# A new order, new engines and new buffers for the same tasks: attention and a gated feed-forward on one core

## The chip, the core and the metric

The kernel runs on one core of a Trainium2 chip. The metric is the time of one execution in microseconds of the device; lower is better. A core has a matrix engine (PE in the profile, with its weight loads as PEld), VectorE (DVE), ScalarE (ACT), GpSimd (POOL) and SyncE (SP), which here only issues transfers. Each works through its own queue of instructions in order; semaphores order them against each other.

## The reference

Four batches of eight heads, 768 positions, head size 64. Heads 0, 2 and 6 see all earlier positions, the other five see 4 first positions and a window of 64. What follows is a gated feed-forward over the 3072 tokens:

```
scores = (q @ k.T) / sqrt(64), masked; a = softmax(scores); attn = a @ v        # per batch and head
x = attn, heads side by side: 3072 x 512
g = x @ w_gate; val = x @ w_val                                                # 512 -> 1536
out = (g * sigmoid(g) * val) @ w_out                                           # 1536 -> 512
```

## The kernel before

The program is cut into 1155 tasks, each a handful of instructions for one engine. Three long strings, planned beforehand, fix everything that the tasks leave open: `ORDER` is the order in which they are issued (so the order in every engine's queue), `WAYS` says for each task which of its allowed engines runs it, and `SLOTS` which buffer of a ring it takes. `Plan.order` reads them:

```
numbers = [DIGITS.index(ORDER[2 * i]) * 62 + DIGITS.index(ORDER[2 * i + 1])
           for i in range(len(ORDER) // 2)]
for t, w in zip(self.tasks, WAYS):
    t.way = t.ways[int(w)]
```

Two numbers in `ORDER` that are no tasks stand for filler matmuls of PE. The eight banks of 512 fp32 that the matmuls write to are one ring for everything: a task's slot is its bank, and it must wait until whoever reads the bank's last tenant is done.

The tasks that the rest speaks of, with the lines under which the profile has them:

- `load q3`, `load x2`, `load g4`: SP fetches 512 KB of q, of v (it is called x) or of a weight into a raw buffer (L352 to L365). `cq`, `ck`, `cx2.0.1`, `wc g4` cast them to 16 bits (L209 on ScalarE, L211 on GpSimd, L215 on VectorE); `cx2.m.j` are the four quarters of one v buffer. Values are kept in tile `vt`.
- `sc5.2`, `ex5.2`, `mask5.1`, `val5.1`, `nm5`: for tile 5 of 128 queries, a unit of scores on PE (matmuls over 64 rows, L570), its exponential on ScalarE (L582), the multiplication by a 0/1 mask (L590, VectorE or GpSimd, two operands in SBUF), the product with the values (PE, L600), the division on VectorE (L607, L608). `sk`, `sv` copy a few rows of keys and values; `tr`, `ev`, `xtr`, `xe`, `dk`, `dq`, `xdma` are transposes and their copies.
- `gate4.3.0`, `tanh`, `vals`, `stt1`, `stt2`: for group 4 of 512 tokens and column block 3 of 12, the gate product (4 matmuls of 512 columns, L762), tanh on ScalarE (L768), and on VectorE the two products that make h (L775, and L781 or L1152). For groups 4 and 5 the val product is made with seven products instead of eight (`wp5.2.4v` are 4 matmuls of 256 columns, L1108), which are put together by `wy` (copies), `wb` (VectorE, L1129) and `wa` (GpSimd or VectorE, L1129).
- `out4.p1` to `out4.p7`: the output product of a group with seven block products (12 matmuls of 256 columns each, L866), again with sums around it. `hs4.x.part` are the sums of blocks of h (L837, 128x768 at 16 bits, both operands in SBUF, VectorE or GpSimd); `oe4.r1`, `c11`, `r6`, `r67`, `r56`, `c12`, `c21`, `c22` gather the products from the banks into `out_sb` (L904, most on VectorE, each adding to what an earlier one left). `st` are the stores.

What each sum of h reads and writes decides who waits for whom:

```
to, a, b, op = {1: (s1, A[1, 0], A[1, 1], ALU.add),
                2: (A[0, 0], s1, A[0, 0], ALU.subtract),
                3: (A[1, 0], A[0, 0], A[1, 0], ALU.subtract),
                4: (A[0, 1], A[0, 1], A[0, 0], ALU.subtract)}[x]
```

`out5.p5` needs both parts of `hs5.1`, `out5.p6` both of `hs5.2`; `hs5.3.1` needs `hs5.1.1`, and `hs5.2.1` needs `hs5.3.1`. The sums for group 4 must have been read before those of group 5 are written.

Of the kernel before, what the change touches and what calls it, by code (L numbers as in the profile page):

```python
# [14 lines left out]

ORDER = (
    "06000307090A01081U1V0D041cxl1W1X0C021d1f0B20211g1e280g1i2229231h2B2A1j0m1r2C0h1Y1p1s2D1a0F1Z2N1q"
    "2X1b2E0G2O051k1l2W1t1m2F1u2L1x1v1w2f2M1n2g1y2cxk2h0n27252d241o262l2i2e2m2G0E0y2H1z2I2P0z2j2Q8m2t"
    "2R0k8w8n102o308x8o2x112p2U312J0i132V8p2K8z2y0H8q918y2k9G928r3C2n94939L2z8s3I9H323D0q9B95968t149I"
    "8u3J903L978v389C0l99983K9D9E0j2Z9M9A9J3M9F2Y9O9N0o3N9K3U339P1C3V3R2a2q2r0I3S2b9p2s16343O2u3W9k9q"  # L20
    "0r3T3P9r35363b9l2v0J3E379V3X3F1D3H3f3i3Q9Q9m3g0s1F9n9R9W3A3h9S9u0p399o9s9v3B9X2w0K9z179t3j0x3Y9w"
    "3Z0M193u9Y3a3G3l9Z3n3c3m9a1G0uA09T3v9bA13o3d0t409U3k2SA23e9c0O43A33p441A3q41459x3r2T0v42490L9y4C"
    "463y4D9f4H4A3w3x9i9g4B479d9h0P9j3s124Q4K3t4N4R9eB74O1HB24LA6BA48B8B5A7B30QB9184EAd4M0w5C1Q4ZBM15"
    "4F4PBBBP4g4G1BAsA8B40RAYAtB60N4YAxAu1KBNAvA94e5D1IBC1RBO1TAeAgAyAf1J5GATAwBD0SB0Az1EBQ5KAUBH4VAh"
    "4I1MBFBE4h5fA4BG1SAZ0T5EAa5IAi1L5FB1AbBI1OAV4J4aAnAc4bBJAC0VA5AB4fAoAA4d4l4o1NAD5gBK1P3zAG4p5nAE"
    "BL4m4S0aAH4TAjAI5JAp4WAk4U4i5L4q4jAM4v4c4n0W4rAJ5H514y4XANAK4zAF5l4k52AWAL4sAO4tAlAS4u4w0U5T54AX"
    "5m5UAq535055APAr6LAm5W565MAQ57BTBRARBU5o5NBV58BW5c594x5XBf5ABS5O5B5v5p5s5Y5w5VBh5q0YBX5t0XBY5Z5r"
    "5a0ZBd5i5b606366Be64BZ6H676w5P6I6N5QCj6K5uCUBaCk6P6EClCPBcCVBg0bCKCQCW745dCm5R7OCLCF73Cn5hBi69CN"
    "5SCMCR5x5yCOC06O615zCXC16J5e6vC2C3685kBq0f6x6572BjBrCYCGC46Q6ACIBl7P5jCHBt71Bs8e6U6RBk6VCe0eBu0c"
    "CA6WCf626SCg6B6CCJChCB6TCCBvCiCSBw6DBb70C5Bx6G6eCTByC66yBpC77F6X6Z0d7GBzC86YCZ7HC96a757CCa6n6FCb"  # L30
    "Bm6o817Q6b6c76CqCDCs826dDf7DBnCc77BoDr7E89CEE1Ds7WDt7879E2DcCdDu7XCrDdE3CtE4De7UDD7A6MCo6gDvDE7L"
    "7RDgDmDF7BCuE5DGDnCp7VDXCvDHDoDI88DYDZ6z7Y6k7bDJ7S6lDKDS7ZDa6m7j7IDb7JDTDp8f7K7cE6Dq6fDU6p7m6hE7"
    "E8E96i7dDN80EA6jDL6q86Dw7M7a7N6r6sDxDOD06t7nDy6u7p7eD1Cw7x7fDM7q8387DP8A7T8D7sCx8ED2Cz7gD3DV8B7o"
    "DhDW7h7rD47i7t7kDiEaD68NDj85D5Cy8G8YD87u8ZD7DQEc8H7vDR8I8W7y7wEtDk8J8C8X8F8T8QDl8K8L8g8UDzEb8hEu"
    "Ee8O7l8RFNE0EfEv7z848i8jD98MDC8VEg8kF0EhDAElEi8SDBEmFl8lEj8PF1EwF8Fm8aEEExFnEG8bEk8cFpEdF98dEpFq"
    "EnEBF2FrEoFAEyEqF4FBEDEzErF3FCEsECFRFsFFFSF5GcFGEFFtFDFTEHFOEJFoFPFZGYEKFUF6FaEIFEF7FVFbGjFQGZFW"
    "ENFcGdGaFuFXFJFvGeGbFYFdFKGfFxFHFeEOFLFwFyGnFfGkEMGrFIGgGsG1FzGlGhHPG2FMGiG0FhG3GtFgFiEPGoHQGuGm"
    "HLELEQGvHRGpH6GqG5FjERFkHSH7HjG6G4ESH8HkH2G7GwETHlHMG8GxEVGyH3HTGzHNH0EWHUEUEZHOHrHVGCH1HmHvH9HW"
    "HsHnGBEXHtHXHoHwHpHDGEH4HqHYHbEYHxHEGDHHH5HcHAHfHuHBHyHFHCHZG9HIHgHdHGGHGFHhHJHaHzGGHKGLGKI0HeGA"
    "GRGIGJI1HiI3I2I9GNI4GMI5GPI6IBGOGUGSIAGQI7GVGTGWINICI8GXIEIDIRIFIHISITIJIGIIILIKIOIUIMIQIXIVIPIa"  # L40
    "IWIYIZIbIc"
)
WAYS = (
    "000000000000000000000000000000000000000000000000000000000000222222202202202021110101101110110120"
    "212101100000000000000000210012022201011011000000000000002100222212001010000000000001001000000000"
    "001200002221000000001001000000001000010010000000000212210100000000010000002000000100000120010010"
    "000000000100000001200000000000000000000000000000000000000000220000001000000000100000210001001000"
    "002101120020000001001000000021000100100000000021020000000000000000010001202200200000001000000002"
    "100000000000012001020000000000000000000200000000000000001100010000000000000000000000000000000000"
    "000000000000000000000000000000000000000000000000000010000010000000000000000000000000000000000000"  # L50
    "000000000000000000000000000000000000000000000001100000000000000000000000000000000000000000000000"
    "000000000000000000000000000100011100100000000000001000000000000000000000000000000000000000000000"
    "000000000000000001001110001000000000001110110000000001000000000000010000000100000000100000000000"
    "000000000000000000000000000000000000000000011110000110000000000010111100000100001000000000000000"
    "000000000000000000000000000000000000000000000000000000000000000000000111000110000000011001011001"
    "000"
)
SLOTS = (
    "00142310557834204A728958195847A05075426281030677515371900124020502261616103140412010360010742002"
    "230141644162600102323204501403026420412050167244160200630522202002012065012304614540136200140030"  # L60
    "240446501210360010203640541636200124622522240461410021100360646216225204112036102200040230524011"
    "754000311261110210650104126300270103022210611241110500540131010000035544525102202260017123601001"
    "134116402151200027401451273542323411351124127310321226025402571046015210141134122541546421225110"
    "511741244025511051263100312340064001500410070060289507A26253604307171403041416110712161035452396"
    "8A20102627386131505051406140110030713108323248"
)
# [1277 lines left out]
```

## Time and profile before

| | |
|---|---|
| time, three runs | 236.64 us median (236.51 to 236.7) |
| span of the profiled execution, first to last instruction | 234.7 us |
| PE busy | 228.7 us, 97% |
| VectorE busy | 204.4 us, 87%; 51.04 of 53 us from 165 to 218 us |
| ScalarE busy | 157.9 us, 67% |
| GpSimd busy | 136.4 us, 58% |
| granted PE clock | 0.999 |

The page gives no other time of the profiled execution than its span; the 1.9 us between span and median lie before the first and after the last instruction of the program. A matmul's duration holds the filling of the array, so consecutive matmuls overlap in the records, and a PE that is busy throughout can still start its matmuls late; the starts tell how densely they are issued.

### The profile page before, as it was taken

What the parts mean: (1) busy time and instruction counts of PE and PEld (TensorE: products, weight loads), DVE (VectorE), ACT (ScalarE), POOL (GpSimd) and SP (SyncE); (2) the same over time, 40 slices, a digit from 0 to 9 for tenths busy, and PEclk for the clock granted to TensorE, in tenths of its full rate; (3) what the DMA queues carried; (4) which work ended last, traced back from release to release, by engine and by line L of the source; (5) the groups of instructions that cost most, each with busy time, mean ns of one, the idle gap of its engine ahead of it and who ended that gap; (6) DMA issues with size and microseconds to landing.
All of it is one profiled execution on the core that took longest, in us unless ns stands there. A gap on an engine that the chain in (4) does not pass through costs nothing.

```text
span 234.7 us, 5854 instructions
## 1 busy us (share of the span) xinstructions
PE 228.7 (97%) x2283; PEld 152.8 (65%) x2283; DVE 204.4 (87%) x369; ACT 157.9 (67%) x256; POOL 136.4 (58%) x150
## 2 busy tenths in 40 slices
PE   7899999999999999999999999999999999999994
PEld 2577865654457778645564556776876767668883
DVE  1889989989989998989879974889979999999954
ACT  3599999679899779856786389768554643553110
POOL 7485499864695300469840887273096930593950
PEclk9999999999999999999999999999999999999999
DMA  6999999999999998998994621500920000220054
GB/s 180 351 343 366 327 340 369 343 341 314 271 259 220 236 251 166 270 179 178 234 217 124 102 45 31 62 3 2 225 45 3 3 0 3 89 89 4 0 201 159
DMA packets 67196, 40.76 MB, mean 174 GB/s; under 512 B 25184, under 2 KB 61024, under 8 KB 67168
## 3 DMA queue, kind: packets, MB, share of 16 engines
q1 hardware_dynamic: 65104, 37.37, 64.5%
q10 hardware_dynamic: 2064, 3.02, 3.6%
q8 instruction: 18, 0.29, 0.5%
q14 instruction: 10, 0.08, 0.1%
HBM read 28.31 MB, written 6.29 MB: 147 GB/s over the span
## 4 chain that ended last, share of the span: by engine, by line
PE 89%; ACT 3%; DMA 2%; DVE 2%; SPq 2%; issue 1%; POOL 0%; ACTq 0%; POOLq 0%
PE banks L762 45%; PE banks L866 23%; PE banks L1108 8%; PE banks L570 6%; PE banks L600 6%; DMA raw<-in_k_dram 2%; ACT e L582 2%; SPq L352 1%; PE banks L476 1%; PE banks L624 1%; DVE xb L608 1%; ACT kT L209 0%; SPq L357 0%; DVE kT L211 0%; DVE sil L775 0%
## 5 line engine op out<-in xcount | busy, mean ns | idle before, releaser
L762 PE MATMUL banks<-xt,wg_sb 128*128 128x512 f16 (+1 forms) x304 | 71.6, 368 | 0.1
L582 ACT ACTIVATE e<-banks 128x1024 f16<-128x1024 f32 (+2 forms) x68 | 59.4, 911 | 11.0 <-PE banks L570 6.3
L768 ACT ACTIVATE sig<-banks 128x512 f32<-128x512 f32 (+1 forms) x76 | 42.8, 577 | 30.6 <-PE banks L762 23.2
L762 PE MATMUL banks<-xt,wv_sb 128*128 128x512 f16 (+1 forms) x208 | 48.2, 363 | 0.0
L762 PEld LDWEIGHTS <-wg_sb 128*128 128x128 f16 x304 | 28.6, 98 | 25.9 <-issue 0.5
L866 PEld LDWEIGHTS <-h_sb 128*128 128x128 f16 x420 | 40.2, 98 | 7.4
L775 DVE SCALAR_TENSOR_TENSOR sil<-sig,banks 128x512 f32<-128x512 f32 (+1 forms) x52 | 32.8, 641 | 5.8 <-ACT sig L768 4.7
L781 DVE SCALAR_TENSOR_TENSOR h_sb<-sil,banks 128x512 f16<-128x512 f32 (+1 forms) x52 | 32.8, 640 | 3.1 <-PE banks L762 2.7
L837 POOL TENSOR_TENSOR h_sb<-h_sb 128x768 f16<-128x768 f16 x13 | 21.3, 1644 | 21.1 <-DVE hs_sb L837 17.2
L762 PEld LDWEIGHTS <-wv_sb 128*128 128x128 f16 x208 | 19.1, 98 | 17.2
L590 POOL TENSOR_TENSOR e<-e,m 128x640 f16<-128x640 f16 (+1 forms) x16 | 26.6, 1670 | 5.7 <-ACT e L582 4.7
L904 DVE TENSOR_TENSOR out_sb<-banks,out_sb 128x512 f32<-128x512 f32 x37 | 25.0, 684 | 2.1 <-PE banks L866 1.7
L866 PE MATMUL banks<-wt_sb,h_sb 128*128 128x256 f16 x216 | 26.0, 273 | 0.1
L866 PE MATMUL banks<-wo_sb,h_sb 128*128 128x256 f16 x204 | 24.9, 273 | 0.0
L209 ACT COPY raw<-banks 128x512 f32<-128x512 f32 x26 | 14.6, 588 | 15.2 <-DVE h_sb L1152 5.5
L570 PEld LDWEIGHTS <-kT 64*128 64x128 f16 x472 | 14.5, 94 | 9.2 <-issue 8.7
L570 PE MATMUL banks<-qT,kT 64*128 64x128 f16 x472 | 19.9, 218 | 0.1
L211 POOL CAST hq<-raw 128x1024 f16<-128x1024 f32 (+1 forms) x9 | 8.0, 893 | 20.1 <-DMA raw<-in_k_dram 18.2
L600 PEld LDWEIGHTS <-e 128*128 128x128 f16 x472 | 17.3, 97 | 3.6 <-POOL e L590 0.3
L600 PE MATMUL banks<-vt,e 128*128 128x65 f16 x472 | 18.6, 193 | 0.0
L608 DVE TENSOR_TENSOR xb<-banks,rc 128x512 f16<-128x512 f32 x24 | 16.6, 691 | 0.8
L775 DVE SCALAR_TENSOR_TENSOR banks<-sig,banks 128x512 f32<-128x512 f32 x24 | 16.3, 687 | 0.2 <-ACT sig L768 0.2
(85 smaller groups left out, 318.6 us busy)
## 6 DMA issues: line engine op xcount, KB each, us to landing
raw<-in_v_dram SPq DMA_DIRECT2D x12, 512.0 KB, 6.8
raw<-in_q_dram SPq DMA_DIRECT2D x8, 512.0 KB, 5.6
...
```

Source lines behind the costliest of these rows:

```text
L570: nc.tensor.matmul(sc[:, c:c + n, :], weights, moving, start=first, stop=last)
L582: nc.scalar.activation(out=to, in_=src, func=AF.Exp, scale=scale)
L590: ENG[task().way].tensor_tensor(out=ev, in0=ev, in1=mm, op=ALU.mult)
L600: nc.tensor.matmul(avs[t][:, odd, n * 66:n * 66 + 65], ee, vv, start=(m == 0), stop=(m == len(bl) - 1))
L608: nc.vector.tensor_tensor(out=xb.rearrange("p n o d -> p o n d"), in0=av[:, :, :, 0:64], in1=rc.to_broadcast([128, 2, 4, 64]), op=ALU.mult)
L762: nc.tensor.matmul(ps, wsb[:, kk, j * 128:(j + 1) * 128], xt[:, kk, c[0]:c[1]], start=(kk == 0), stop=(kk == 3))
L768: nc.scalar.activation(out=sg[g, j, c], in_=gs[g, j, c], func=AF.Tanh, scale=0.5)
L775: nc.vector.scalar_tensor_tensor(out=sl[g, j, c], in0=sg.pop((g, j, c)), scalar=1.0, op0=ALU.add, in1=gs.pop((g, j, c)), op1=ALU.mult)
L781: nc.vector.scalar_tensor_tensor(out=hs[g, j][:, c[0]:c[1]], in0=sl.pop((g, j, c)), scalar=0.5, op0=ALU.mult, in1=vs.pop((g, j, c)), op1=A ...
L837: ENG[T_hs[g, x][part].way].tensor_tensor(out=to, in0=a, in1=b, op=op)
L866: nc.tensor.matmul(rooms[g, p][:, x, lo:hi], left[:, j, 128 * x:128 * x + 128], right[:, j, lo:hi], start=(on is None and (j == 0 if apart ...
L904: nc.vector.tensor_tensor(out=cell(*to), in0=room, in1=plus, op=ALU.add)
```

## The change

All 1155 tasks and the 9 filler matmuls stay; what each computes stays. Of the 1155 tasks 146 change their engine, 502 of the 622 buffers are another one, and the order changes everywhere from the 151st entry on. Sums with two operands in SBUF: 27 go from VectorE to GpSimd and 29 from GpSimd to VectorE. The diff is three strings; its first lines:

```
-    "2X1b2E0G2O051k1l2W1t1m2F1u2L1x1v1w2f2M1n2g1y2cxk2h0n27252d241o262l2i2e2m2G0E0y2H1z2I2P0z2j2Q8m2t"
+    "2X1b2E0G2O051k1l2W1t1m2F1u2L1x1v1w2f2M1n2g1y2czY2h0n27252d241o262l2i2e2m2G0E0y2H1z2I2P0z2j2Q8m2t"
...
-    "8u3J903L978v389C0l99983K9D9E0j2Z9M9A9J3M9F2Y9O9N0o3N9K3U339P1C3V3R2a2q2r0I3S2b9p2s16343O2u3W9k9q"
+    "8u3J903L978v9C99989E389O0o3K9A2Z9D9F0J9M3M2Y2q2r9N9P3N332s3R0l0r9J342a3S9K2u1C169p9q9r3W3X3F3O2b"
```

Read as names, these are the pieces that the text below needs. The first 150 entries keep their order, except that the 72nd, a filler of 4 matmuls, writes another bank (7 instead of 0); near the start the engines change: before the first gate ScalarE gains `sv0.1` (from GpSimd) and `xe0` (from VectorE), and gives `evq2.0` to VectorE and `cx1.1.0` to GpSimd.

PE around the first score units of tiles 5 and 6, where `|` stands where 64-row score matmuls begin or end:

```
before: vals0.2.256 vals0.3.0 vals0.3.256 | sc6.2 sc5.2 sc6.1 | val4.1 val4.0 gate0.9 | sc6.0 sc6.3 | gate0.8
after:  vals0.2.256 vals0.3.256 val4.1 val4.0 | sc5.2 sc6.1 | vals0.3.0 gate0.9 | sc6.3 sc6.0 sc6.2 | gate0.8
GpSimd before: sk0.3 cx2.0.1 cx2.0.0 wc_g4 cx2.1.1 wc_g2
GpSimd after:  wc_v1 cx2.0.1 cx2.0.0 cx2.1.0 wc_g4 wc_g2
```

The loads up to `load x3` are issued in the same order as before. From the first gate on, PE changes to 64-row score matmuls and back 25 times before and 23 times after.

The end, from the last split products on:

```
PE before: out4.p1 out4.p2 wp5.2.3v gate5.10 out4.p6 out4.p5 gate5.11 out4.p7 out4.p4 out4.p3 out5.p1 out5.p5
           out5.p2.0 out5.p6 out5.p7 out5.p4 out5.p2.1 out5.p3.0 out5.p3.1
PE after:  out4.p1 wp5.2.5v gate5.4 gate5.5 gate5.10 wp5.2.3v out4.p2 wp5.2.4v gate5.11 out4.p5 out4.p7 out4.p6
           out4.p3 out4.p4 out5.p1 out5.p5 out5.p6 out5.p7 out5.p4 out5.p2.1 out5.p3.0 out5.p3.1 out5.p2.0
VectorE before: stt1_5.10 stt2_5.5 stt2_5.10 oe4.r6 stt1_5.11 stt2_5.11 oe4.r67 oe4.r56 oe4.c21 oe4.c12 oe4.c22
                hs5.3.1 hs5.2.1 hs5.2.0
VectorE after:  wb5.2.c12v stt1_5.10 stt2_5.10 stt1_5.4 stt2_5.4 stt1_5.5 stt2_5.5 stt1_5.11 stt2_5.11 oe4.c11
                hs5.1.1 oe4.r6 oe4.r67 oe4.r56 oe4.c12 oe4.c21 oe4.c22 hs5.2.0 hs5.2.1 oe5.r1 hs5.4.0 hs5.4.1
GpSimd before:  hs4.4.1 hs4.4.0 hs5.1.0 hs5.3.0 hs5.1.1 hs5.4.0 hs5.4.1
GpSimd after:   hs4.2.0 wa5.2.c11v hs4.2.1 hs4.4.1 hs4.4.0 hs5.1.0 hs5.3.0 hs5.3.1
```

The last product is then `out5.p2.0`, gathered by ScalarE (`oe5.c11.0`, 256 columns) and stored from ScalarE's queue; before it was `out5.p3.1`, gathered by VectorE and stored from SP's. Banks at the end, after: `out5.p1` takes banks 2 and 3 (bank 3 had `out4.p7`), `out5.p5` takes 6 and 7 (they had `out4.p3` and `out4.p4`).

In VectorE's queue a task stands right behind one whose result it reads 19 times before and 54 times after; from `wp4.1.1v` on (the first split product) 9 and 24 times.

More of the change, by code (lines that the diff above doesn't have):

```diff
@@ L21 @@
[L21 to L40, printed above, removed]
@@ L41 @@
-    "IWIYIZIbIc"
+    "8u3J903L978v9C99989E389O0o3K9A2Z9D9F0J9M3M2Y2q2r9N9P3N332s3R0l0r9J342a3S9K2u1C169p9q9r3W3X3F3O2b"
+    "3P3U9k3T0I35363b9l3E371D9V3V179W9m9Q0j3H3f9X3i3j3g390p0u9n9o9s9T3Q9t3Y3Z0K9R3v9S9Y1F9zA03a3k9U3l"
+    "3h1GA1193n3u3o0x9Z4344A2A39u3c9v0t3m9x452v2w9w9y400O3G1A413A3B423p8e3q3r9a2S46494C9b9c9d9e0L4A4D"
+    "474H9f9g3s2T3t3d3e3z9i9h9jA64Q4R1H0s0N4N4O483x0w4K4VAd0vAeA7AxAf154LBCBD0M5C3wAyBFBEBG3y4B4YAzBM"
+    "AgA90TAhBNBOBP5J0P1EBQ4eB74E0c4F1O4f4G12BHBIBJ1M1N181Q1R4P4ZB8BAB94gAvB0BKBBBL0S1B1I0Q4IAsAt0R4M"
@@ new lines @@
+    "B1B2Au5i4JB3Ai4dATAUB55D5LAw1P5KAV4S0b4T4UB4B6AjA4A5AlAkAm5gAWAX1JA84W4i4o4p4l4hAn1TAYAZAq4XAA0Y"
+    "4aAaAbAc1KAoApAr4vAC4jABAD4m4n5fAG5152AH5H4q4r5n5T1SAI0U5U1L4b4k4s4c5IAJ4t4u5l53AK4y4zAL5M5455AF"
+    "AM0WAE5W5cAO56576MBR50AP5XBT8gBU4w5F58BV5hBX59ANAQ7P4x5ABZ5N0XASBS5vBW5p5q5wAR8f5s605t5EBY5V5Y6H"
+    "BfBdBaBe5B0a6v5oCUCVCW5rCFCGCHBvBgBw0ZCICJBx0VC5C65mC7C8C9716N6OByBz5O5P725Q5RC0C1C3C2C45G5Z5a5b"
+    "CX7T6w5uCjCm8h5j0e6I6P6670CY69Bc63CkCl6ECn5k7Q6465CZCaCPCQCA67CRCbCcCd0dBqCD5d685x6ACBCCBrBs5y61"
@@ new lines @@
+    "6Q736x5zCEBtBuCeCfCg6R6S0f74Bb5S6UCKCL62CMBhBi6V7X6B6C7O8k8lCS6D5e6e6G6n6oCT6X7F7U7G6T816KChCi6J"
+    "BjBl6Y6W6Z6a7C75CN6FCOBmBk6b6c8088DcCrBnCq76DdDIDeDf7HDg7D7E6dBoDJDK77DrDLDsE66y78Dt84DME1E27LDp"
+    "797AE7E9BpE8EAE37RDm6gDnDwCs85Do7W6k7V6l7YDuDv6f7ZDxDyCoCu6h6iDq7b7jCwCpCx6z7ICtCv8iDS7J7KE47ME5"
+    "7cDD7dDTDU7S6p8786DEDF7m6q7p896m6j7N7xD0D1D2D36L6r6s6t6uD4Cy7n8D8A7q7eD57fDz8NE07a7B7g7h7i8EDXDY"
+    "DV82DW8BDaDZDND67sDbDO7rDP7k8Y7t8G8F7oDh7u7vCz8Z7wDGDHEtEaEu8j8H8I8JD88C8T8UEcEbEdEeElEfDkDQEmEv"
@@ new lines @@
+    "DR83F0D7EgEwDiExF8F9DjEnDlF1FFFGDC7y8K8L8OF2D9EhFAEi8MEjDAFB8QEDEy8R7lDB8WEpEqEk8VFCFJFHEzF38XEE"
+    "FDErFVFWEsFKFXFYFNFOEo7zFZFaFPFQG5FLFMG6G78SF4FEFIFtFb8a8b8cFdF5FpFeFuFcFf8PFRG8FSFTEBECFvEJEGEI"
+    "EFFq8dFUEKGcGdF6FgFrF7FwFxFsFhFiFyFzGjEHELERGkFjFkGYG0EMENEPEOG1G2GZGbGrGsHPFlFmG3G4GtHQGeEQFnET"
+    "EUHLGuGlGaGvFoGfGwGgGhH2ESEVGyH3H6HMGzGiHNHRGBGmHSGnH7GoHjHkEWHlHDH8H4HOGpH5GDEZH9HAHvHwHTGqH0Hm"
+    "HUEXHxHyEYGCGEHEGxHVH1HWHXHBHrHnHsG9GFHtHFHuGGHYHZHHHIHoHpHqHaHbHfHzI0HJHKGHGKI1I2HcHCHdHGHeI3GJ"
@@ L42 @@
+    "GRHgHhHiGNI4I5I6GLGAGII9IAGMGOGUGSGVGWIBGPGQI7ICGTGXINIDIEI8IHIFIGIJILIIIUIKIOIQIMIPIVIWIXIYIaIb"
+    "IZIcIRISIT"
 )
 WAYS = (
[L44 to L52, printed above, removed]
@@ L53 @@
-    "000000000000000001001110001000000000001110110000000001000000000000010000000100000000100000000000"
-    "000000000000000000000000000000000000000000011110000110000000000010111100000100001000000000000000"
-    "000000000000000000000000000000000000000000000000000000000000000000000111000110000000011001011001"
+    "000000000000000000000000000000000000000000000000000000000000222102222002222200221011000000100000"
+    "222101100000000010000000220002022222011011000000000000001100222222011010000001000001001000000000"
@@ new lines @@
+    "002101002121000000000000000000020000000000000000000202100100000000010000002000100000000120002200"
+    "000000000000000002100000000000000022102200000010000000001000210002022000000100000000220000001000"
+    "001201011200000001000000000021000000000000000220020000000100000000010000102002220000001001000000"
+    "100000000000021001000200000000000000000020001001000000001011111100000000000000000000000000000000"
+    "000000000000000000000000000000000000000000000000000001010000000000000000000000000000000000000000"
@@ new lines @@
+    "000000000000000000000000000000000000000000010001100000000000100000000000000000000000000000000000"
+    "000000000000000000000000000000110000000000000000011000000000000000000000000000000000000000000000"
+    "000000000000000011111110010000000000000010100001000000000000100010000100000001000000000000000000"
+    "000000000000000000000000000000000000000000011111100110000000000001101100000000000000001000000000"
+    "000000000000000000000000000000000000000000000000000000000000000000001101100000000000001001010000"
@@ L58 @@
 SLOTS = (
[L59 to L65, printed above, removed]
+    "193204751A36723497219A6737716025547A6945821014A096350A004124202206015603340323626444120430610445"
+    "616041230245613146341000364022025503410002426532002320550421511343226420121005323322025061151140"
+    "031521335026104400123032520516004543545260410322210241102021343110533141232510255136061540230518"
+    "920411750255004101321070025711311024012210371147004301720237125702246747040121601770107100010141"
+    "252003101210160121012071267067645212661113002200560131000512720044127312770173002067520120030014"
+    "70257110212340257011011711261127600051146415307137522443205A606115100403141112110602071245371617"
+    "46506373515A4021405171305131403020610027951461"
 )
```

## The prediction

> **What bounds the kernel now.** I read the first lines of the page, then the busy time by stages, then the chain of work that ended last.
>
> ```profile
> span 234.7 us, 5854 instructions
> PE 228.7 (97%) x2283; PEld 152.8 (65%) x2283; DVE 204.4 (87%) x369; ACT 157.9 (67%) x256; POOL 136.4 (58%) x150
> ...
> 20.00:66.00 46.00, 46.00 (x477) 28.12 (x476) 43.32 (x86) 41.21 (x67) 33.22 (x38) 1.00 1.13 331
> 165.00:218.00 53.00, 53.00 (x418) 38.68 (x416) 51.04 (x87) 26.13 (x48) 29.90 (x22) 1.00 0.17 47
> 218.00:232.00 14.00, 13.40 (x122) 11.66 (x120) 10.87 (x19) 1.56 (x3) 8.10 (x6) 1.00 0.34 122
> ...
> 203.53 3.45 PE banks L762 x16
> 218.30 13.11 PE banks L866 x120
> ```
>
> In the stage rows the numbers after the length are PE, weight loads, VectorE, ScalarE and GpSimd. From 20 us to the last matmul PE is busy throughout, at a granted clock of 1.00. The two pieces of the chain say how densely: 16 matmuls of 512 columns in 3.45 us are 0.216 us each, 120 of 256 columns in 13.11 us are 0.109 each. So a gate costs 0.864, an output product of 12 matmuls 1.31, a split product of 4 matmuls 0.436. The work itself is the same after the change. What an order can still give is small: the switches between kinds of matmul, and the few starts that come late. What it can cost is open upwards: any new wait on PE is paid in full, since nothing behind it is idle. VectorE is the second bound, with 1.96 us idle in the 53 before 218.
>
> Two views of PE in order of time show both kinds of loss:
>
> ```profile
> 108.64 1.89 PE L762 MATMUL banks<-xt,wv_sb 128*128 128x512 f16 x8
> 110.46 0.62 PE L570 MATMUL banks<-qT,kT 64*128 64x128 f16 x16
> 111.01 0.39 PE L762 MATMUL banks<-xt,wg_sb 128*128 128x512 f16 x1
> ...
> 104.78 1.67 PE L762 MATMUL banks<-xt,wv_sb 128*128 128x512 f16 x7
> 106.47 0.81 PE L762 MATMUL banks<-xt,wg_sb 128*128 128x512 f16 x3
> ```
>
> Eight matmuls from 108.64 on end their issue at 108.64 + 1.73 = 110.37; the scores start at 110.46, so entering the 64-row form costs 0.09 to 0.10. Sixteen scores take 0.55 until the next gate starts at 111.01. I put the bare scores at 0.028 each, 0.45 in all, an estimate from these rows between nothing and 0.55/16, which leaves 0.10 for the way out. One excursion thus costs 0.20 (0.10 to 0.25 as bounds). The other pair shows a real wait: seven matmuls from 104.78 end at 106.29, the next starts at 106.47, 0.18 later. I found one more of about 0.15 (near 150 us).
>
> **The change, part by part.** The sum is made against the profiled span of 234.7; the median of the runs is 1.9 us above it and is moved by the same amount.
>
> *Start to the first gate.* ScalarE's exponentials set the pace there.
>
> ```profile
> 17.40 0.59 ACT L209 COPY qT<-banks 128x512 f16<-128x512 f16 x1
> 17.87 0.62 ACT L209 CAST vt<-raw 64x512 f16<-64x512 f32 x1
> ...
> 15.08 0.96 POOL L211 COPY vt<-vt 2x330 f16<-2x330 f16 x2
> ```
>
> It loses the copy of 0.59 and the cast of 0.62, and takes the two small copies that GpSimd had (0.96) and `xe0` (a copy of a bank, 0.59 like the first row). That is 1.21 out and 1.55 in, but the cast stood behind a wait and the fillers cover PE; by the queue the exponential before the first gate moves by less than 0.1. I take -0.1, bounds -0.2 and +0.3.
>
> *`val4` moved ahead of scores.* PE reaches it earlier; what it needs doesn't come earlier.
>
> ```profile
> 27.00 1.91 PE L762 MATMUL banks<-xt,wv_sb 128*128 128x256 f16 x16
> 28.84 0.84 PE L570 MATMUL banks<-qT,kT 64*128 64x128 f16 x20
> 30.29 1.04 PE L762 MATMUL banks<-xt,wg_sb 128*128 128x512 f16 x4
> ...
> 27.62 1.27 POOL L211 CAST vt<-raw 64x512 f16<-64x512 f32 x2 [0.31 <-DMA raw<-in_v_dram]
> 29.19 1.04 POOL L211 CAST wg_sb<-raw 128x1024 f16<-128x1024 f32 x1 [0.31 <-DMA raw<-in_moe_w_gate_dram]
> ```
>
> The 16 matmuls from 27.00 are four `vals` pieces of 0.44. After the change three stand there, so PE comes to `val4.1` at 28.31. `val4` needs `cx2.0.0` and `cx2.0.1`, the two GpSimd casts that start at 27.62 because the transfer of `x2` lands then, and end at 28.89. The loads ahead of `x2` keep their order and the transfer engines were kept busy, so it lands no earlier. PE waits 0.6. Next in GpSimd's queue `cx2.1.0` now stands ahead of `wc g4`: 0.63 more, so the gate weights are cast from about 29.6 to 30.6 instead of 29.19 to 30.23. `gate0.9` stood at 30.29 before; behind a `val4` that ends 0.6 late it starts at about 30.8 and no longer feels the cast. Against the small wait for that cast before I take +0.55. Upper bound 0.7; lower bound 0, if `x2` should land earlier.
>
> *Two excursions fewer*, 23 instead of 25 from the first gate on: 2 x 0.20 = -0.4 (bounds -0.2 and -0.5).
>
> *Waits of before* (0.18 and 0.15): the order at both places is another one. I take half away, -0.15, bounds -0.33 and 0; nothing says that the new order has none of that size.
>
> *The end.* Times here count from the end of the issue of `gate5.11`. PE: `wp5.2.3v` ends at -2.61, `out4.p2` at -1.30, then 0 to 6.55 the five products `out4.p5 p7 p6 p3 p4`, `out5.p1` to 7.86, `out5.p5` to 9.17, `out5.p6` from 9.17. What VectorE and GpSimd need per step:
>
> ```profile
> 217.16 1.28 DVE L1152 SCALAR_TENSOR_TENSOR h_sb<-banks,raw 128x512 f16<-128x512 f32 x2
> ...
> 219.01 0.70 DVE L775 SCALAR_TENSOR_TENSOR banks<-sig,banks 128x512 f32<-128x512 f32 x1
> 219.75 0.69 DVE L1152 SCALAR_TENSOR_TENSOR h_sb<-banks,raw 128x512 f16<-128x512 f32 x1
> 220.35 3.20 DVE L904 TENSOR_TENSOR out_sb<-banks,out_sb 128x512 f32<-128x512 f32 x5
> ...
> 217.27 1.03 PE L762 MATMUL banks<-xt,wg_sb 128*128 128x512 f16 x4
> 218.38 0.60 ACT L768 ACTIVATE sig<-banks 128x512 f32<-128x512 f32 x1 [2.46 <-PE banks L762]
> ...
> L837 POOL TENSOR_TENSOR h_sb<-h_sb x13: 1634/1643/1653, 58.7 to 219.7; 128x768 f16<-128x768 f16 x13
> L837 DVE TENSOR_TENSOR h_sb<-h_sb x9: 545/549/558, 61.1 to 223.5; 128x768 f16<-128x768 f16 x9
> ```
>
> Two independent steps of VectorE take 1.28, so the second starts 0.60 behind the first. `stt2` behind the `stt1` it reads starts 0.74 later (219.01 to 219.75). A consumer starts 0.25 behind the issue end of a product (217.27 + 0.86 = 218.13 against 218.38). A sum of h is 0.55 on VectorE and 1.64 on GpSimd, 1.60 from start to start.
>
> GpSimd: `hs4.4.1` needs `out4.p2`, so -1.05; `hs4.4.0` 0.55, `hs5.1.0` 2.15, `hs5.3.0` 3.75 to 5.39. VectorE: `wb5.2.c12v` at -2.36, then `stt1_5.10` -1.76, four pairs at 0.74 + 0.60 each, `oe4.c11` at 3.60, `hs5.1.1` at 4.20. So `hs5.1.1`, a sum with both operands in SBUF, arrives while `hs5.3.0`, another one, runs on GpSimd. What that means the trace shows twice:
>
> ```profile
> L1129 POOL TENSOR_TENSOR raw<-raw x5: 1272/1277/1725, 172.5 to 209.7; 128x512 f32<-128x512 f32 x5
> L1129 DVE TENSOR_TENSOR raw<-raw x1: 1186/1186/1186, 171.9 to 171.9; 128x512 f32<-128x512 f32 x1
> ...
> 171.88 1.19 DVE L1129 TENSOR_TENSOR raw<-raw 128x512 f32<-128x512 f32 x1
> ...
> 171.37 1.15 POOL L1088 TENSOR_TENSOR raw<-xt,raw 128x512 f16<-128x512 f16 x1
> 172.48 1.73 POOL L1129 TENSOR_TENSOR raw<-raw 128x512 f32<-128x512 f32 x1
> ...
> 159.77 1.52 DVE L590 TENSOR_TENSOR e<-e,m 128x1024 f16<-128x1024 f16 x2
> ...
> 158.70 1.64 POOL L1058 TENSOR_TENSOR raw<-wv_sb 128x768 f16<-128x768 f16 x1
> ```
>
> VectorE's sum of 171.88 ends at 173.07, 0.55 behind the end of GpSimd's at 172.52: it waited for that end. GpSimd's next one, 172.48, took 1.73 where its like takes 1.28: it waited for VectorE's. And the two masks of 159.77 take 1.52 while GpSimd's sum runs to 160.34. So `hs5.1.1` runs from 5.39 to 5.94. Behind it on VectorE stand the gathers, four of them each reading the one before: `r6` 5.86, `r67` 6.60, `r56` 7.34, `c12` 8.08, `c21` 8.68 to 9.37, `c22` 9.42, `hs5.2.0` 10.02 to 10.57, `hs5.2.1` to 11.04. `out5.p5` needs the banks that `c12` and `c21` free (unhindered 7.86), and `out5.p6` waits for `hs5.2.0` and, 0.33 later, `hs5.2.1`: it starts at 10.6 instead of 9.17. I take +1.45. If `hs5.1.1` gets in first, everything is 1.19 earlier and 0.3 are left; the bounds are 0 and 1.6.
>
> Here a rule of the Trainium skill speaks the other way. "VectorE: DVE Perf Modes", section "The DRAIN you can't avoid", says that eight copies take the same time with a semaphore behind each as with one behind the last, so a step that reads the one before it would cost nothing extra. The rows above differ: 0.74 against 0.60. By the page the four pairs are 0.56 shorter, `hs5.1.1` comes at 3.64, ahead of `hs5.3.0`, and the sum would be about 236.7 instead of 238.1.
>
> *The last store.* ScalarE's copy is shorter than VectorE's, its store slower:
>
> ```profile
> 225.96 0.37 ACT L209 COPY out_sb<-banks 128x256 f32<-128x256 f32 x1 [1.79 <-DMA out_dram<-out_sb]
> 231.43 0.42 DVE L896 TENSOR_TENSOR out_sb<-banks,out_sb 128x256 f32<-128x256 f32 x1 [0.23 <-PE banks L866]
> ...
> out_dram<-out_sb ACTq DMA_DIRECT2D x3, 128.0 KB, 2.1
> ...
> out_dram<-out_sb SPq DMA_DIRECT2D x1, 128.0 KB, 1.8
> ```
>
> -0.05 for the copy, up to +0.3 for the landing, which was taken among other stores: +0.1, bounds -0.05 and +0.3.
>
> *Two-operand sums elsewhere.* Only five of VectorE's 57 overlap one of GpSimd's instructions at all before; the two shown cost VectorE half a microsecond each, where PE didn't wait. So keeping them apart is worth nothing on the path: 0, up to +0.5 where one lands in the wrong place.
>
> Sum: -0.1 + 0.55 - 0.4 - 0.15 + 1.45 + 0.1 = +1.45, so a span of 236.2 and a time of **238.1**.
>
> **The rivals.**
>
> *`hs5.1.1` arrives first* (about the same). Its place is the start of `hs5.3.0` at 3.75; the margin is 0.45. For it: VectorE has room between the pairs if `wb5.2.c12v` starts earlier, and by the page's rule it does come first. Against it: both queues hang on PE and the durations vary by 0.01. With 0.3 left at the end, 236.64 + 1.45 - 1.45 + 0.3 = 236.9; with nothing left 236.6.
>
> *Faster: PE only loses switches.* The place is PE between 20 us and the end. Nothing new waits: `x2` lands 0.6 earlier, or other work of the order fills the gap, and the end holds. -0.1 - 0.4 - 0.33 = -0.8, so 235.8. It decides where all new waits of PE together stay under 0.35. For it: bare chains between PE tasks (product, tanh, `stt1`, `stt2`, bank free) have 0.2 us or more to spare everywhere. Against it: the landing row above.
>
> *Slower still: VectorE's backlog.* 15 more neighbours that read each other from the first split product on, at 0.14 each, are 2.1 us against 1.96 idle in that stage. Where they meet, PE waits for banks: up to +0.8 more, 238.9.
>
> *No change at all* (order and engines neutral): the same numbers as the first rival.
>
> **How the numbers follow.** Forecast 0.47; backlog on top 0.08; first rival 0.25; faster 0.20. 0.2% is 0.47 us, about what a measurement of this kernel can tell from no change: faster is below 236.17, slower above 237.11. So faster 0.20, same 0.25, slower 0.55. The likeliest case alone lies between 237.4 (a tail of 0.8) and 238.6; the range must reach to both other signs: 236.0 to 238.8.
>
> **What the profile after would show.** In order of time: `val4` at about 28.9 with a gap before it on PE; 23 excursions; `hs5.1.1` on VectorE as an L837 row of well over 0.55 while GpSimd's L837 runs; PE with gaps ahead of `out5.p5` and `out5.p6`; VectorE at more than 51 of 53 us before the end. It is wrong if L837 on VectorE stays at 0.55 in the end, if PE's last products run 12 by 12 without a gap, or if `val4` starts at 28.3.

## The result, and the profile after

The changed kernel takes **251.28 us** (median of four runs, 250.42 to 251.82) against 236.67 us (236.51 to 236.73): ratio 1.0615, 95% interval 1.0594 to 1.0635. That is 14.6 us slower. The forecast was 238.1 with a range of 236.0 to 238.8: the sign was right, the size was not. The profiled execution took 250.42 us, with a span of 248.5.

The page of the changed kernel, its first lines, then PE's waits by what released them:

```profile
span 248.5 us, 5850 instructions
PE 233.1 (94%) x2283; PEld 153.1 (62%) x2283; DVE 215.0 (87%) x367; ACT 155.3 (62%) x250; POOL 151.7 (61%) x158
```

```profile
PE banks L762 <- DVE sil L775: 4.7, 4, 2.9
PE banks L866 <- DVE h_sb L837: 2.3, 2, 2.0
...
PE banks L866 <- DVE sil L775: 1.0, 1, 1.0
PE banks L866 <- DVE out_sb L904: 0.7, 1, 0.7
PE banks L600 <- DVE e L590: 0.3, 1, 0.3
PE banks L762 <- DVE out_sb L904: 0.3, 1, 0.3
```

Before, this view has no row behind the start. Now PE stands still for VectorE at places from 24 us to the end. The columns are microseconds, times and the longest one; they count from the modelled end of a matmul, so the true loss is a little larger. It can be had from the starts: each matmul should start 0.216 us (512 columns), 0.109 (256), 0.030 (values) or 0.028 (scores) behind the one before it, and what it is later is a switch of form, a wait (over 0.055), or a slow clock (twice the spacing). From the first gate to the last matmul:

| | before | after |
|---|---|---|
| switches to and from scores | 5.32 (25 excursions) | 4.65 (23) |
| waits | 0.84 | 12.83 |
| matmuls at twice their spacing | 0 | 2.73 |
| rest | 1.37 | 1.29 |
| start of the last matmul | 231.12 | 245.06 |

The four differences add up to +13.97; the last matmul starts 13.94 later, and the first gate 0.05 earlier. The waits by place: 0.72 at 24 us, 0.33 up to 39, 1.11 at 56, 3.32 at 66 to 72, 1.31 at 79 to 82, 3.08 at 98 to 107, 1.19 at 168 to 172, 1.62 in the end, 0.15 elsewhere.

VectorE has nearly the same work (330 tasks, 334 before), and is busy 10.6 us longer. Where, the groups by form show (after the bar the busy time in us, then the mean of one in ns). Two rows of the kernel before, then the changed one; before, the masks of 128x640 read 482 and the sums of h 549:

```profile
L590 DVE TENSOR_TENSOR e<-e,m 128x1024 f16<-128x1024 f16 x14 | 9.9, 714 | 0.0
L415 DVE TENSOR_TENSOR wt_sb<-wo_sb,wt_sb 128x512 f16<-128x512 f16 x2 | 0.8, 418 | 0.0
```

```profile
L590 DVE TENSOR_TENSOR e<-e,m 128x1024 f16<-128x1024 f16 x13 | 13.3, 1024 | 0.4 <-ACT e L582 0.4
L590 DVE TENSOR_TENSOR e<-e,m 128x640 f16<-128x640 f16 x11 | 7.0, 635 | 0.0
L837 DVE TENSOR_TENSOR hs_sb<-h_sb 128x768 f16<-128x768 f16 x7 | 5.8, 847 | 0.0
L415 DVE TENSOR_TENSOR wt_sb<-wo_sb,wt_sb 128x512 f16<-128x512 f16 x5 | 5.1, 1015 | 0.1
```

All of them are sums with two operands in SBUF; the instructions that read a bank kept their lengths (L775 682, L904 684). Taken one by one, 28 of 59 such sums lie beside an instruction of GpSimd, 21 are longer than alone, by 15.9 us together. Before it was 4 of 57, and two, by 0.94. The other engine is held up as well: GpSimd is busy 151.7 us in the changed kernel, and 146.6 where VectorE's sums are replaced (the first experiment below). The first of the 21 in order of time:

```profile
22.71 1.40 POOL L590 TENSOR_TENSOR e<-e,m 128x640 f16<-128x640 f16 x1
22.99 1.66 DVE L590 TENSOR_TENSOR e<-e,m 128x1024 f16<-128x1024 f16 x1
...
24.57 0.41 DVE L775 SCALAR_TENSOR_TENSOR sil<-sig,banks 128x256 f32<-128x256 f32 x1
...
25.04 0.38 PE L762 MATMUL banks<-xt,wg_sb 128*128 128x256 f16 x2 [0.55 <-DVE sil L775]
```

`mask4.0` starts on VectorE at 22.99 and stands until about where GpSimd's `mask4.1` ends (24.11): 1.66 us instead of 0.68. The `stt1` behind it empties a bank late, and PE's next gate waits. The longest wait:

```profile
62.35 2.31 POOL L590 TENSOR_TENSOR e<-e,m 128x1024 f16<-128x1024 f16 x1
...
64.02 0.92 DVE L415 TENSOR_TENSOR wt_sb<-wo_sb 128x512 f16<-128x512 f16 x1
...
65.17 1.12 POOL L211 CAST hq<-raw 128x1024 f16<-128x1024 f32 x1 [0.52 <-DMA raw<-in_k_dram]
...
65.31 1.26 DVE L415 TENSOR_TENSOR wt_sb<-wo_sb 128x512 f16<-128x512 f16 x1
66.24 0.80 POOL L211 CAST vt<-raw 64x512 f16<-64x512 f32 x1
...
66.61 1.83 DVE L415 TENSOR_TENSOR wt_sb<-wo_sb,wt_sb 128x512 f16<-128x512 f16 x1
67.01 1.15 POOL L415 TENSOR_TENSOR wt_sb<-wo_sb 128x512 f16<-128x512 f16 x1
...
68.77 0.68 DVE L775 SCALAR_TENSOR_TENSOR sil<-sig,banks 128x512 f32<-128x512 f32 x1
...
69.49 1.01 PE L762 MATMUL banks<-xt,wg_sb 128*128 128x512 f16 x2 [2.86 <-DVE sil L775]
```

Three sums of weights, 0.42 each alone, take 0.92, 1.26 and 1.83: each has to let an instruction of GpSimd end, casts of one operand as well as sums. `stt1 1.8.0`, whose bank PE wants, stands behind them. Around the end of this wait the slow clock begins, and again around that of the 2.1 us wait at 101; the stage rows (PE, weight loads, VectorE, ScalarE, GpSimd, then the granted clock):

```profile
64.00:66.20 2.20, 2.20 (x12) 0.98 (x10) 2.17 (x4) 2.13 (x4) 1.68 (x2) 1.00 1.20 285
69.50:72.10 2.60, 2.60 (x7) 0.95 (x7) 2.52 (x5) 0.68 (x2) 0.00 (x0) 0.50 1.19 307
...
102.90:106.60 3.70, 3.70 (x14) 1.97 (x15) 3.70 (x3) 0.00 (x0) 3.51 (x4) 0.54 0.99 206
```

### The profile page after: what moved, and what is told of

It reads as the page before. It is cut to its first block, busy times and chain, and to the rows that moved or that the text cites. A ratio compares the mean times of both kernels' runs of the same rounds, so it can differ in the third digit from the quotient of the medians.

```text
span 248.5 us, 5850 instructions
## 1 busy us (share of the span) xinstructions
PE 233.1 (94%) x2283; PEld 153.1 (62%) x2283; DVE 215.0 (87%) x367; ACT 155.3 (62%) x250; POOL 151.7 (61%) x158
## 4 chain that ended last, share of the span: by engine, by line
PE 68%; DVE 23%; issue 3%; DMA 2%; SPq 1%; ACT 0%; DVEq 0%; ACTq 0%
PE banks L762 32%; PE banks L866 15%; PE banks L1108 7%; PE banks L570 6%; PE banks L600 5%; DVE sil L775 3%; DVE e L590 3%; DVE wt_sb L415 3%; DVE out_sb L904 3%; DVE h_sb L781 2%; DVE h_sb L837 2%; DMA raw<-in_k_dram 2%; DVE hs_sb L837 2%; PE banks L476 1%; DVE xb L608 1%
## 5 line engine op out<-in xcount | busy, mean ns | idle before, releaser
L762 PE MATMUL banks<-xt,wg_sb 128*128 128x512 f16 (+1 forms) x304 | 72.5, 376 | 5.0 <-DVE sil L775 4.7
L762 PE MATMUL banks<-xt,wv_sb 128*128 128x512 f16 (+1 forms) x208 | 47.7, 363 | 0.0
L775 DVE SCALAR_TENSOR_TENSOR sil<-sig,banks 128x512 f32<-128x512 f32 (+1 forms) x52 | 32.7, 640 | 5.9 <-ACT sig L768 5.8
L590 POOL TENSOR_TENSOR e<-e,m 128x640 f16<-128x640 f16 (+1 forms) x14 | 25.9, 1855 | 5.5 <-ACT e L582 5.0
L866 PE MATMUL banks<-wt_sb,h_sb 128*128 128x256 f16 x216 | 26.6, 278 | 2.3 <-DVE h_sb L837 2.3
L904 DVE TENSOR_TENSOR out_sb<-banks,out_sb 128x512 f32<-128x512 f32 x37 | 25.2, 684 | 2.7 <-PE banks L866 2.2
L837 POOL TENSOR_TENSOR h_sb<-h_sb 128x768 f16<-128x768 f16 x14 | 23.3, 1667 | 1.8 <-PE banks L866 0.7
L837 POOL TENSOR_TENSOR h_sb<-hs_sb,h_sb 128x768 f16<-128x768 f16 x6 | 9.8, 1640 | 23.2 <-PE banks L866 18.3
L590 DVE TENSOR_TENSOR e<-e,m 128x1024 f16<-128x1024 f16 (+1 forms) x24 | 20.1, 846 | 0.4 <-ACT e L582 0.4
L211 POOL CAST vt<-raw 64x512 f16<-64x512 f32 x27 | 17.3, 643 | 3.6 <-DMA raw<-in_v_dram 2.3
L209 ACT COPY raw<-banks 128x512 f32<-128x512 f32 x24 | 13.3, 594 | 7.7 <-PE banks L1108 7.7
```

The lines of the kernel that those rows point to most:

```text
L590: ENG[task().way].tensor_tensor(out=ev, in0=ev, in1=mm, op=ALU.mult)
L762: nc.tensor.matmul(ps, wsb[:, kk, j * 128:(j + 1) * 128], xt[:, kk, c[0]:c[1]], start=(kk == 0), stop=(kk == 3))
L775: nc.vector.scalar_tensor_tensor(out=sl[g, j, c], in0=sg.pop((g, j, c)), scalar=1.0, op0=ALU.add, in1=gs.pop((g, j, c)), op1=ALU.mult)
L837: ENG[T_hs[g, x][part].way].tensor_tensor(out=to, in0=a, in1=b, op=op)
L866: nc.tensor.matmul(rooms[g, p][:, x, lo:hi], left[:, j, 128 * x:128 * x + 128], right[:, j, lo:hi], start=(on is None and (j == 0 if apart ...
L904: nc.vector.tensor_tensor(out=cell(*to), in0=room, in1=plus, op=ALU.add)
```

## The experiments

**VectorE's two-operand sums replaced by one-operand copies of the same length.** The deciding edit, in the changed kernel and in the one before:

```
+    def twosum(way, out, in0, in1, op, read):
+        if way == "DVE":
+            nc.vector.tensor_reduce(out=out.bitcast(FP), in_=read.bitcast(FP).unsqueeze(len(read.shape)),
+                                    axis=mybir.AxisListType.X, op=ALU.max)
+        else:
+            ENG[way].tensor_tensor(out=out, in0=in0, in1=in1, op=op)
-        ENG[T_hs[g, x][part].way].tensor_tensor(out=to, in0=a, in1=b, op=op)
+        twosum(T_hs[g, x][part].way, out=to, in0=a, in1=b, op=op, read=...)      # and so for L590, L415, L1058, L1088
```

> The changed kernel with one edit: each sum with two SBUF operands that VectorE runs (59 of them: masks L590, sums of h L837, of weights L415 and L1058, of x L1088) is replaced by a copy of one operand, bit for bit, as a reduction over half as many 32-bit elements, which lasts as long as the sum does alone (384 elements for 128x768 at 16 bits, 0.55 us). The masks and the sums are left out so; order, engines, buffers, GpSimd's work and the load of VectorE stay. Theory (VectorE's two-operand sums are held up while GpSimd works: 21 of them were 15.9 us longer than alone, and PE's 12.8 us of waits and 2.9 us at half clock hang on those): the waits at 24, 56, 66, 82, 101, 107, 168 and 235 us go, the clock stays full, and the time falls from 251.3 to 236.5-238. Rival (the new order gives PE too little slack behind VectorE's queue, blocked or not, since VectorE is as loaded as before): the time stays above 247.

> The same edit in the kernel before (57 sums of VectorE replaced by one-operand copies of the same length, so masks and sums are left out). Theory: only two of its sums are longer than alone, by 0.94 us together, and neither held PE up, so the time stays within 0.4 us of 236.67 (236.2 to 236.9). Rival (the one-operand copies are cheaper in themselves): it falls by over 1 us as well.

The changed kernel falls to **242.68 us** (240.88 to 243.42; ratio to before 1.0265, 1.0248 to 1.0282). The kernel before stays: 236.85 (1.0005, 0.9996 to 1.0014); there 56 sums are copies, and the 57th, VectorE's L1129, stays a sum. So the copies aren't cheaper, and the hold-ups, those of GpSimd and the slow clock behind them included, cost 8.6 us; but 6.0 remain, which the theory did not expect. Part of these goes with the clock: the two runs with a granted clock of 1.00 took 240.88 (the profiled one) and 241.83, the three with 0.993 took 242.68 to 243.42. PE's waits of this kernel (lines behind the edit stand 7 higher; the copies are L215):

```profile
PE banks L577 <- DMA kT<-hq: 0.8, 1, 0.8
PE banks L873 <- DVE h_sb L215: 0.6, 1, 0.6
PE banks L607 <- POOL vt L211: 0.6, 1, 0.6
PE banks L577 <- DMA qT<-hq: 0.5, 1, 0.5
...
PE banks L607 <- ACT e L589: 0.4, 1, 0.4
```

The waits for `stt1` and `out_sb` are gone, and new ones have come in view: PE waits for transposing transfers, by the starts 1.04 us at 80.0 and 0.74 at 85.9, and for `val4`'s casts, 0.73 at 28.7. In the changed kernel PE was late there already: `sc11.1`, which waits for `dk5.1` here, starts 6 us behind the landing there (86.36 against 80.35).

**The same for the early sums alone** (`if way == "DVE" and len(running) < 351`).

> The changed kernel with that edit only for the sums issued before ws3.1, that is those that start before 61.9 us (mask4.0, mask8.0, hs0.1.1 are the held-up ones among them; 2.65 us of 15.9). The later sums are the real ones. Theory A (the first hold-ups shift VectorE and GpSimd against each other, and the later collisions come from that shift): without them the later sums keep apart as well, and the time falls to 237-241. Theory B (each collision stands by itself in the order): only the waits up to 56 us go (0.72 + 0.16 + 1.11), and the time is about 249.3 (248.5 to 250).

248.51 us (247.26 to 249.41), 2.8 less than the changed kernel: theory B, at the lower end of its range. The waits of 66, 82, 101, 107, 168 and 235 us are all still there (3.46, 1.22, 2.11, 0.45, 0.60, 0.87 us). The collisions behind them are built into the order; a later one doesn't need the early ones. Part of the 2.8 is the clock: here it is slow for one stretch (granted 0.993 in all four runs), in the changed kernel for two (0.986 in all four).

**The cost by itself.** Four instructions of VectorE of one kind, beside GpSimd idle, casting or summing; for instance

```
def d_two(a, b, n):
    nc.vector.tensor_tensor(out=a[:, 0:768], in0=a[:, 0:768], in1=b[:, 0:768], op=ALU.add)
def p_cast():
    nc.gpsimd.tensor_copy(out=p_a, in_=p_f)
```

> None of the reference's work: twelve stages on their own, four instructions of VectorE each, of one of four kinds (a sum of two SBUF operands 128x768 at 16 bits; a one-operand reduction of 384 32-bit elements; a sum of a PSUM bank and an SBUF operand, 128x512 at 32 bits; a plain copy 128x1024 at 16 bits), with GpSimd idle, casting (128x1024, one operand, 1.04 us each, back to back) or summing (128x768, 1.64 us each). Theory (any SBUF work of GpSimd holds up a VectorE instruction with two SBUF operands, and only such): the sums take 0.55 us with GpSimd idle and 1 us or more beside casts and beside sums; reductions and sums from a bank take the same in all three (0.55 and 0.69). Rival (only GpSimd's own two-operand sums do it): beside casts the sums stay at 0.55. The plain copy has no row in the two traces that tells: either.

Its groups by form, named by the pair (`d_two` two SBUF operands, `d_red` one-operand reduction, `d_bank` bank and SBUF, `d_copy` plain copy):

```profile
L50 DVE TENSOR_TENSOR d_two_p_sum_a<-d_two_p_sum_a,d_two_p_sum_b 128x768 f16<-128x768 f16 x4 | 6.2, 1543 | 3.9 <-ACT d_two_p_sum_b L72 3.8
L61 DVE COPY d_copy_p_sum_a<-d_copy_p_sum_b 128x1024 f16<-128x1024 f16 x4 | 5.8, 1451 | 3.9 <-ACT d_copy_p_sum_b L72 3.8
L50 DVE TENSOR_TENSOR d_two_p_cast_a<-d_two_p_cast_a,d_two_p_cast_b 128x768 f16<-128x768 f16 x4 | 5.1, 1263 | 10.0 <-ACT d_two_p_cast_b L72 9.9
L61 DVE COPY d_copy_p_cast_a<-d_copy_p_cast_b 128x1024 f16<-128x1024 f16 x4 | 4.2, 1061 | 0.4 <-ACT d_copy_p_cast_b L72 0.3
...
L57 DVE TENSOR_TENSOR d_bank_p_sum_a<-banks,d_bank_p_sum_b 128x512 f32<-128x512 f32 x4 | 2.8, 692 | 5.1 <-ACT d_bank_p_sum_b L72 5.0
L50 DVE TENSOR_TENSOR d_two_p_idle_a<-d_two_p_idle_a,d_two_p_idle_b 128x768 f16<-128x768 f16 x4 | 2.2, 558 | 1.5 <-ACT d_two_p_idle_b L72 1.4
...
L53 DVE TENSOR_REDUCE d_red_p_sum_a<-d_red_p_sum_b 128x384 f32<-128x384 f32 x4 | 2.2, 553 | 5.7 <-ACT d_red_p_sum_b L72 5.6
L61 DVE COPY d_copy_p_idle_a<-d_copy_p_idle_b 128x1024 f16<-128x1024 f16 x4 | 1.7, 427 | 5.2 <-ACT d_copy_p_idle_b L72 5.1
```

In its one execution the theory holds for the sums: 0.56 us alone, 1.26 beside casts, 1.54 beside sums (the first of these four came before GpSimd and took 0.56, the others 1.87), while reductions and sums from a bank don't feel GpSimd. The two engines take turns, instruction by instruction: each of VectorE's sums waits for the running cast to end, and GpSimd's next cast, 1.04 us alone, takes 1.25. The plain copy suffers too (0.43 to 1.06 and 1.45), which the theory had left open. The Trainium skill says this on the page "SBUF — State Buffer", section "Who interferes with whom": a VectorE instruction with two SBUF inputs contends with a GpSimd instruction that reads SBUF, one in a two-port mode (a copy can be) contends with GpSimd, and whoever issues first has the shared ports for its whole instruction while the other is blocked. The runs agree, and give the prices.

**Two transposes moved forward in SP's queue**, in the kernel with one-operand copies. As names:

```
-dq5.1 dk5.0 loadk7 loadx6 loadq7 xdma8 dk6.1 dk6.0 loadk10 dk5.1 xdma9 loadk9 dk7.0 loadq8 dq6.0 dq7.0
+dq5.1 dk5.0 dk5.1 dq6.0 loadk7 loadx6 loadq7 xdma8 dk6.1 dk6.0 loadk10 xdma9 loadk9 dk7.0 loadq8 dq7.0
```

> The changed kernel with VectorE's two-operand sums replaced by one-operand copies of the same length (as in after_one: masks and sums left out), and two entries of SP's queue moved forward: the transposing transfers dk5.1 and dq6.0 right behind dk5.0, ahead of the loads k7, x6, q7, k10, k9, q8. In after_one PE waited 1.04 us at 80.0 for dk5.1 (landed 81.02) and 0.74 at 85.9 for dq6.0 (landed 86.60), though what they transpose had been cast at 65. Theory (part of what is left of the loss, 6.0 us, is SP's new order, which lets these transposes stand behind loads that nobody needs yet): both waits go, with what hangs on them (an exponential 0.54, a sum of h 0.76), and the time falls from 242.7 to 239-241. Rival (the transfer engines are full, so somebody is late anyway): it stays at 242 or more.

242.14 us (241.59 to 242.88): the rival. In the profiled run the two waits go, and another comes. ScalarE's row in order of time, and PE's waits:

```profile
75.26 1.04 ACT L207 CAST hq<-raw 128x1024 f16<-128x1024 f32 x1 [3.59 <-DMA raw<-in_k_dram]
```

```profile
PE banks L767 <- ACT e L587: 3.5, 1, 3.5
```

`load k7` now lands at 75.16 instead of 71.15; its cast stands on ScalarE ahead of an exponential, and PE waits 3.7 us for that one's bank. So in both orders somebody is late; whether a third order would serve all was not tried.

**The transposes left out.** Of the 28 transposing transfers of q and k all but `dk5.0` and `dk5.1` are dropped, in three kernels (so 26; the expectations say 21 of 23):

```
     def dmat(n, kd, m):
+        if kd == "q" or n > 5:
+            return
```

> As after_one (the changed kernel with VectorE's two-operand sums replaced by one-operand copies of the same length), and 21 of the 23 transposing transfers of q and k are left out (all but dk5.0 and dk5.1); the scores of the later tiles read older q and k, so nothing waits for them and the transfer engines and SP's queue are lighter. Theory (what is left of the loss in after_one, 6.0 us, is mostly the supply: the new order of SP's queue brings transposes, and loads whose casts stand ahead of exponentials on ScalarE, too late): 238-239.5, with runs that scatter by less than 0.6 us; 0.7 us of the rest is the wait of val4 for x2's casts at 28 us. Rival (what is left is VectorE's and ScalarE's queues being in a tighter order): 241 or more.

> The same two edits in the kernel before, for comparison (one-operand copies for VectorE's two-operand sums, 21 transposing transfers left out). Theory: no PE work of it waits for a transpose, so it stays at 236.4-237.0. Rival (the lighter transfers help any order): 236.2 or less.

> The changed kernel with its real sums, and those 21 transposing transfers left out. Theory (the two causes share their waits: where PE is late through a held-up sum, the transposes have come in time): 250-251.5, so without the transposes the sums cost all but some 2 us of the loss. Rival (the causes add up): the 3 to 4 us that after_one loses by the supply come off here too, 247-248.5.

| us | before, copies | after, real sums | after, copies |
|---|---|---|---|
| all transposes | 236.85 | 251.28 | 242.68 |
| 26 left out | 236.64 | 248.35 | 237.89 |

The first two forecasts hold: 237.89 us (237.66 to 238.3; ratio 1.0048, 1.0032 to 1.0064), a small scatter, no gain in the kernel before. The third was a miss: 248.35 (248.3 to 249.72), the rival's number. The hold-ups cost 8.6 to 10.5 us (251.28 to 242.68; 248.35 to 237.89), the transposes 2.9 to 4.8, together 13.4 of 14.6. Both hold a share of slow clock. With real sums three of the four runs without transposes had one slow stretch (0.992) where the changed kernel had two; the fourth had two (0.986) and took 249.72, so at an equal clock 1.6 of the 2.9 are left. With copies, at the full clock, the transposes cost 3.0 to 3.9 (240.88 and 241.83 to 237.89). With real sums PE waited for no transpose, in either trace: there they cost by shifting other waits, and how was not followed. Of the last 1.2, PE's waits in this profile (lines 9 higher) show `val4`'s casts and one sum of h:

```profile
PE banks L875 <- DVE h_sb L215: 0.6, 1, 0.6
PE banks L609 <- POOL vt L211: 0.5, 1, 0.5
```

**Engines alone and order alone.** One string of the change each time: the new `WAYS` with the old `ORDER` and `SLOTS`, and the reverse; then the first of them with one-operand copies.

> The engines alone: order and buffers of the kernel before, each task on the engine that the changed kernel gives it (146 tasks differ, 56 of them two-operand sums). Theory (what costs is that two-operand sums of VectorE and work of GpSimd fall together, and only the exact times of a whole plan keep them apart): the old order no longer keeps them apart, over 10 of VectorE's sums are held up, by 5 us or more together, and the time is above 241. Rival (the loss is in the new order of PE, and the engines, nearly the same work on each, are neutral): 236-238.

> The order alone: order and buffers of the changed kernel, each task on its engine of the kernel before. Theory (as for the engines alone): held-up sums again, 5 us or more together, time above 241. Rival (the loss is in the engines chosen, 27 sums and ten more casts on GpSimd): it falls back to 236-239.

> As before_ways (order and buffers of the kernel before, engines of the changed one, 256.1 us), with VectorE's 59 two-operand sums replaced by one-operand copies of the same length (masks and sums left out). Theory (there too the held-up sums are most of the loss: 21 of them, 14.3 us longer than alone): 240-247. Rival (an order made for other engines loses by itself: PE reaches tasks before the engine that now has the work ahead of them): above 250.

256.06 us (255.33 to 256.89) with the engines alone, 277.77 (275.64 to 279.34) with the order alone; both are worse than the whole change. 21 sums are held up by 14.3 us in the first, 13 by 10.3 in the second. Without the hold-ups the first falls only to 249.89 (249.84 to 249.95), between the two forecasts: 6.2 of its 19.4 us. In that trace PE still waits 13.6 us by the starts, for masks on GpSimd, `stt1` on VectorE and copies on ScalarE among others. That an order made for one set of engines makes another set wait for each other would explain it, but why those tasks came late was not followed. So these runs don't tell whether order or engines "did it"; either without the other is worse than both.

**One collision alone.** In the kernel before, one digit of `WAYS`: `mask4.1` from VectorE to GpSimd.

> One part alone: in the kernel before, mask4.1 goes from VectorE to GpSimd, as in the change; the first 150 entries of the order are the same, so VectorE's mask4.0 meets it at 23 us. Theory: mask4.0 takes about 1.66 instead of 0.68 us, PE waits about 0.7 us near 24 us for a bank, VectorE is spared 0.48 us of work, later sums are not thrown together, and the time is 237.0-237.6. Rival 1 (one collision shifts the queues and draws others behind it): above 238.5. Rival 2 (hidden): 236.5-236.9.

```profile
23.11 1.72 DVE L588 TENSOR_TENSOR e<-e,m 128x1024 f16<-128x1024 f16 x1
```

The mask is held up as forecast (1.72 instead of 0.68; lines 2 lower), PE waits 0.35, 0.23 and 0.18 us between 24 and 30, and yet the time is 236.81 (1.0002, 0.9993 to 1.0011), no change: rival 2. PE is later by then, and the waits of the kernel before at 106 and 150 us (0.17 and 0.28) are gone in this profile. So the slack of the other tasks paid for this one collision; it did not pay for 21.

## Why the prediction was wrong

**"Two-operand sums elsewhere: 0, up to +0.5".** This is the step that failed; the runs put 8.6 to 10.5 us there. The prediction knew the mechanism, quoted the rows for it, and priced one collision of it at the end. For the rest it took the rarity of overlaps in the trace of before as a property of the work. It was a property of the order: GpSimd is busy 58% of that span, so of 57 sums thrown in anywhere some 33 would have met it, and 4 did (the prediction says five; two of the four met it for less than 0.1 us). A new order had to be followed through both queues for every sum, as was done for `hs5.1.1`, or else be priced as a throw. As an estimate, with 59 sums, GpSimd busy 61%, and the 0.57 us that each of the 28 which met GpSimd lost on average (15.9 over 28), a throw would cost VectorE 20 us; with the measured 15.9 the new order did a little better than that.

**"0.2 us or more to spare everywhere"**, said for the faster rival, was not read from rows. Taking each PE task's start before against the end of the last thing that it needs, 57 of 325 tasks have less than 0.2 us and 152 less than 0.5. So a hold-up of 0.4 to 1.9 us on VectorE (17 of the 21 lie there) often reaches PE, above all where several follow each other; behind those at 90, 119, 140 and 156 us PE waited 0.1 us at most.

**SP's queue behind `load x3`** was not costed: the prediction stopped at "the loads ahead of `x2` keep their order". Loads of v (`x7`, `x10`) and of k (`k10`) had moved ahead of transposes. Leaving the transposes out took 2.9 to 4.8 us off the changed kernel and nothing off the one before. That the new places in the queue make them late is read from the traces (`dk5.1` lands at 70.4 before, 81.0 in the changed kernel with copies); no run put the old order of SP's queue back.

**The clock** was taken as 1.00. After two of the waits it wasn't, and 2.73 us went there in the profiled run, over a sixth of the loss.

**The end: right.** Times from the end of the issue of `gate5.11`, forecast and measured: `hs5.1.1` arrives 4.20, 4.18; `hs5.3.0` on GpSimd 3.75 to 5.39, 3.93 to 5.57 (so the margin by which the likeliest case beat its first rival was 0.25, not 0.45); `hs5.1.1` ends 5.94, 5.98; `c22` 9.42, 9.46; `hs5.2.0` ends 10.57, 10.62; `out5.p6` starts 10.6, 10.67. In order of time:

```profile
231.72 1.64 POOL L837 TENSOR_TENSOR h_sb<-h_sb 128x768 f16<-128x768 f16 x1
...
231.98 1.80 DVE L837 TENSOR_TENSOR hs_sb<-h_sb 128x768 f16<-128x768 f16 x1
...
233.70 4.25 DVE L904 TENSOR_TENSOR out_sb<-banks,out_sb 128x512 f32<-128x512 f32 x6
...
236.68 1.47 PE L866 MATMUL banks<-wt_sb,hs_sb 128*128 128x256 f16 x12 [0.70 <-DVE out_sb L904]
...
237.86 1.02 DVE L837 TENSOR_TENSOR h_sb<-hs_sb,h_sb 128x768 f16<-128x768 f16 x2
...
238.47 4.25 PE L866 MATMUL banks<-wt_sb,h_sb 128*128 128x256 f16 x36 [0.32 <-DVE h_sb L837]
```

`hs5.1.1` takes 1.80, the gathers follow without a break, PE waits 0.87 us before `out5.p5`, 0.48 before `out5.p6` and twice 0.13: 1.62 against +1.45; with the copies 0.21 is left there. As the prediction read the Trainium skill ("VectorE: DVE Perf Modes", section "The DRAIN you can't avoid") `hs5.1.1` would have come at 3.64; the trace disagrees, and the 0.74 of the rows was the right price.

**`val4`: right, but hidden.** 0.55 was forecast; in the changed kernel PE was 0.7 late by then through `mask4.0` and waited 0.17, in the two kernels with copies 0.73 and 0.66. **Excursions:** 23, as said; the switches fell by 0.67 instead of 0.4: two fewer are 0.4, and the others cost 0.20 each instead of 0.21 (5.32 over 25, 4.65 over 23). **Start:** the first gate 0.05 earlier (-0.1 forecast). **The last store:** from the last matmul's end to the end of the span 3.20 instead of 3.29, where +0.1 was said. **VectorE at more than 51 of 53 us** was wrong: 48.2, since PE set the pace later.
